# Row maxima of the scores for eight of 32 units: two key blocks as one difference, a ScalarE relu and one VectorE pass

## The chip, the cores and the metric

The kernel runs on one core of one Trainium2 chip. The engines that matter here are TensorE (PE in the profile; its weight loads are PEld), VectorE (DVE), ScalarE (ACT) and GpSimd (POOL). The metric is the device time of one execution in microseconds; lower is better. A difference is stated as a ratio of the time after to the time before.

## What is computed

The reference is a transformer block on 2048 tokens of width 512: a modulated layer norm, attention with 32 query heads of 16 columns each that share one key and one value head, an output projection with a gated residual, a second modulated layer norm, and a gated linear unit of width 1792 with a second gated residual. The part that the change touches is the softmax:

```python
q = (x @ wq).reshape(B, S, H, Dh).transpose(0, 2, 1, 3)
k = x @ wk
v = x @ wv
scores = jnp.einsum("bhqd,bkd->bhqk", q, k) * (Dh ** -0.5)
p = softmax(scores, axis=-1)
o = jnp.einsum("bhqk,bkd->bhqd", p, v)
```

The softmax needs, for every row of scores (one query of one head against all 2048 keys), the row's maximum before the exponentials are taken.

## The kernel before

**Units.** Attention is cut into 32 units (`NU`): four blocks of 512 queries, and in each block eight groups of four heads. Of the four heads two lie in partitions 0 to 63 (`a = 0`) and two in partitions 64 to 127 (`a = 1`) of the tiles that hold queries (`sst`) and keys (`kst`); the index `p` tells the two heads of one half apart. A matmul on one half uses 48 or 50 of the 64 rows there, so that a matmul of half 0 and one of half 1 can run at the same time.

**Row maxima.** They are computed a unit ahead. For each half, each head pair index `p` and each of four row groups of 128 queries (`r = 4p + t`, eight in all), the scores against a key block of 512 keys (`kc`, four of them) go into one PSUM bank (`max_mm`, tile `mx`), and VectorE takes the maximum of each row with one `tensor_reduce` (line 573) into a column of `mpart`. `max_slots(u)` lists a unit's work as slots, and each slot has one list of operations for each half. In units 1 to 31 a unit has 32 slots with one operation of kind "one" in each half. When a unit's slots are through, `max_fin` reduces `mpart` to the maxima `mm`, TensorE transposes them into `mxt` (line 597), ScalarE and VectorE split them into two fp16 rows `mt` (lines 602 and 603), and a DMA puts those under the queries in `sst`, so that the score matmul of the exponentials subtracts the maximum by itself.

Unit 0 already does it in another way. Its key blocks 2 and 3 are taken as max(s2, s3) = s2 + relu(s3 - s2). A "diff" operation puts two matmuls into one bank: the queries against `kng`, the negated keys of block 2 (a slice of the tile `kwb`), and against block 3. ScalarE writes the positive part into the tile `rel` (line 576). A "both" operation then computes s2 in another bank, and one VectorE instruction adds `rel` and reduces the sum to its maximum (line 578, a custom instruction followed by the read of its accumulator).

**Turns.** The main loop `attend` takes two turns at a time; there are 16 turns in a unit, one for each block of 128 keys. In a turn ScalarE takes four exponentials of 128x512 (`qk_exp`: a score matmul on line 620 into the tile `sc`, the exponential on line 622 into `P`), and four operations of the maxima are issued. The turn ends with `pv`, the product of the previous turn's exponentials with the values: eight matmuls on line 631 that use all 128 rows. The order inside a turn is written out by hand in strings: `NO_SIDE` when there is nothing else to compute, `FEW` when halves of a query projection (`side` on line 484 with the weights `wq`) are laid between, `MANY` for the other projections. `e0` is an exponential's matmul of half 0, `m0` a maxima slot of half 0, `x1` a side half. In `FEW` one turn takes the maxima of one half alone, four slots in a row of `r`, and the next turn those of the other; in `NO_SIDE` each turn takes two slots of both halves. The side matmuls accumulate groups of 24 halves in one bank, and after a group's end ScalarE evicts it (`qf`, line 513).

The first 30 slots of the maxima are issued before the first turn (`LEAD`), together with the loads, norms and keys. Unit 1 begins with the last six of them. The maxima of unit 8 end some 125 turns after that, so units 1 to 8 lie mostly in block 0 of the attention: first 86 turns in `FEW` order, then turns in `NO_SIDE` order.

**PSUM banks.** There are eight. `ps_mx` and `ps_sc` take the bank at the front of a queue and put it back at the end at once, so that score tiles and maxima tiles go round in a ring over all banks that nothing else holds. A matmul into a bank waits for whoever read its previous content. `pv` holds one bank for a unit, a side group one until it is evicted, and short jobs (`mxt`, sums of squares of weights on line 915) one for part of a turn.

Of the kernel before, what the change touches and what calls it, by code (L numbers as in the profile page):

```python
# [23 lines left out]
UB = H // 4  # L24
# [15 lines left out]

CHANNEL = {0: KC - 1, 3: 0, 4: 1, 6: 2}
LOW = -3.0e38
SYNC = mybir.DependencyInfo(mybir.DependencyClass.Sync, mybir.DependencyReason.DATA)


# [9 lines left out]
def adaln_mqa_glu_kernel(ctx: ExitStack, tc: tile.TileContext, x_in, wq_in, wk_in, wv_in, wo_in,  # L55
# [412 lines left out]
    class Group:  # L468
# [22 lines left out]
        def half(self, r):  # L491

            mm = self.put(r, r + 1)
            if self.rows not in (None, r):
                tc.add_manual_dep(mm.ins, sync["before"], SYNC)
            self.rows, self.turn, sync["due"] = r, now[0], True
# [30 lines left out]
    def load_q(u):  # L527
        b, g = divmod(u, UB)
        d = qd[b, g // 2].rearrange("(h e) l n -> e h l n", e=16)
        s = sst[u % 3]  # L530
        h0 = 4 * (g % 2)
        for a in range(2):
            for r, hl in ((0, 0), (1, 0), (2, 1)):
                nc.sync.dma_start(s[64 * a + 16 * r:64 * a + 16 * r + 16, :, :], d[:, h0 + a:h0 + a + 3:2, hl, :])
# [3 lines left out]
    def max_slots(u):  # L538


        if u == 0:
            slots = [[[("one", r // 4, r % 4, kc)] for _ in range(2)] for kc in range(2) for r in range(8)]
            for r in range(8):
                for a in range(2):
                    slots[-1][a].append(("diff", r // 4, r % 4, 2))
                slots.append([[("both", r // 4, r % 4, 2)] for _ in range(2)])
            return slots
        return [[[("one", r // 4, r % 4, kc)] for _ in range(2)] for kc in range(4) for r in range(8)]

    flat = [(u, i, last, step) for u in range(NU) for steps in [max_slots(u)]  # L550
            for i, step in enumerate(steps) for last in [i == len(steps) - 1]]
# [3 lines left out]
    def max_parts(u):  # L555
        if u < NU and u not in mparts:
            mparts[u] = work.tile([128, 2, 2, 4, 4], F32, name="mpart")
            if u == 0:
                nc.vector.memset(mparts[u], LOW)

    def max_mm(u, a, op):
        kind, p, t, kc = op
        s = sst[u % 3]
        m = ps_sc() if kind == "diff" else ps_mx()
        keys = [kst[:, kc * 512:(kc + 1) * 512]]
        if kind == "diff":
            keys = [kng, kst[:, (kc + 1) * 512:(kc + 2) * 512]]
        for i, w in enumerate(keys):
            nc.tensor.matmul(m, s[64 * a:64 * a + 48, p, t * 128:(t + 1) * 128], w[64 * a:64 * a + 48, :],  # L569
                             start=(i == 0), stop=(i == len(keys) - 1))  # L570
        part = mparts[u][:, a, p, t, kc:kc + 1]
        if kind == "one":
            nc.vector.tensor_reduce(part, m, axis=AX.X, op=OP.max)  # L573
        elif kind == "diff":
            r = rel[a] = work.tile([128, 512], F32, name="rel", tag="x1", bufs=6)
            relus.append(lambda: nc.scalar.activation(r, m, AF.Relu))
        else:
            nc.vector.tensor_tensor_reduce(out=rel[a], in0=m, in1=rel[a], scale=1.0, scalar=LOW, op0=OP.add,
                                           op1=OP.max, accum_out=part)

    def drain_relus():
        for f in relus:
            f()
        relus.clear()
# [3 lines left out]
    def max_fin(u):  # L588
        mms[u] = work.tile([128, 2, 8], F32, name="mm")
        nc.vector.tensor_reduce(mms[u], mparts[u].rearrange("p a q t k -> p a (q t) k"), axis=AX.X, op=OP.max)  # L590

    def max_rows(u):
        def f():
            mms[u, "b"] = ps_hold("mxt")
            p = mms[u, "b"][0:16, 0:128]
            mms[u, "p"] = p
            nc.tensor.transpose(p, mms[u].rearrange("p a c -> p (a c)"), ident)  # L597

        def g():
            p = mms[u, "p"]  # L600
            mt = [work.tile([16, 128], F16, name=f"mt{hl}") for hl in range(2)]
            nc.scalar.activation(mt[0], p, AF.Copy, scale=1.0 / 32.0)
            nc.vector.scalar_tensor_tensor(mt[1], p, 1.0 / 32.0, mt[0], op0=OP.mult, op1=OP.subtract)
            ps_give(mms[u, "b"])
            s = sst[u % 3]
            for hl in range(2):
                nc.sync.dma_start(s[48 + hl:113 + hl:64, :, :], mt[hl])
        return [(100, f, g)]
# [428 lines left out]
    def drain_posts():  # L1037
        todo = posts[:]
        posts.clear()
        if tick[0] is not None:  # L1040
            tick[0] += 1
            todo += timers.pop(tick[0], [])
        for f in todo:
            f()

    def max_half(a):
        n = mstep[a]
        mstep[a] += 1
        if n >= len(flat):
            return  # L1050
        u, i, last, ops = flat[n]
        max_parts(u)
        for op in ops[a]:
            max_mm(u, a, op)
        if a == 0:
            return
        if 0 < u < NU - 1 and i == QPRE:
            load_q(u + 1)
        if i == 12:
            max_parts(u + 1)  # L1060
        if last:
            max_fin(u)
            (_, f, g), = max_rows(u)
            later[mstep[1] + 1] = (f, g)

    def late_max():
        for at in [m for m in later if m <= mstep[1]]:
            f, g = later.pop(at)
            f()
            posts.append(g)  # L1070
            return True
        return False
# [7 lines left out]
    def open_gate(step):  # L1080
        if not fill:
            return False
        gate, group = fill[0]
        if not all(g.ended() for g in group.needs):
            return False
        if gate[0] == "h2":
            return gate[1] in h2done
        return gate[0] <= step
# [30 lines left out]
    def side_half(r, cur=cur):  # L1119
        while True:  # L1120
            if not cur:
                if cur is not second and second and second[0].turn != now[0]:
                    cur.append(second.pop())
                elif open_gate(now[0]):
                    cur.append(fill.popleft()[1])
                else:
                    return
            if not cur[0].ended():
                break
            cur.clear()  # L1130
        if cur[0].did[r] < cur[0].n:
            cur[0].half(r)

    def attend(u, kt):


        now[0] = u * NSTEP + 2 * kt
        if cur and cur[0].ended():
            cur.clear()
        side = cur[0] if cur else fill[0][1] if open_gate(now[0]) else None  # L1140
        style = NO_SIDE if side is None else FEW if side in qs else MANY
        order = [(w[0], int(w[1])) for w in style.split()]
        count = {}
        for turn in range(2):
            now[0] = u * NSTEP + 2 * (kt + turn)
            sync["before"] = sync["exp"]
            drain_posts()
            for j, (what, a) in enumerate(order):
                if j == len(order) // 2:
                    drain_posts()  # L1150
                    late_max()
                    hooks(u, 2 * (kt + turn))
                a = a if style is NO_SIDE else a ^ turn
                if what == "m" and mstep[a] >= len(flat) and style is MANY:
                    mstep[a] += 1
                    side_half(a, second)
                elif what == "m":
                    max_half(a)
                elif what == "x":
                    side_half(a)  # L1160
                else:
                    k = count[a] = count.get(a, -1) + 1
                    qk_exp(u, kt + (k // 2 if style is MANY else turn), k % 2, a)
            assert not sync["due"]
            for g in ended:
                g.finish()
            ended.clear()
            for f in ends:
                f()
            ends.clear()  # L1170
            v = u * KT + kt + turn - 1
            if v >= 0:
                pv(*divmod(v, KT))
                if v % KT == KT - 1:
                    ends.append(lambda: pv_out(u - 1))
            if not late_max() and turns:
                _, f, post = turns.popleft()
                f()
                posts.append(post)
            hooks(u, 2 * (kt + turn) + 1)  # L1180
# [22 lines left out]
    for u in range(NU):  # L1203
        if u == 1:
            side.extend(dlist)
        for kt in range(0, KT, 2):
            attend(u, kt)
# [8 lines left out]
    u = NU - 1  # L1216
# [62 lines left out]
```

## Time and profile before

| | |
|---|---|
| time, median of 3 runs (lowest to highest) | 1686.23 us (1686.07 to 1686.28) |
| time of the profiled execution | 1688.73 us |
| its span, first to last instruction | 1686.7 us |
| PE busy | 1661.1 us, 98% of the span |
| DVE busy | 1389.7 us, 82% |
| ACT busy | 1217.1 us, 72% |
| POOL busy | 517.2 us, 31% |
| chain that ended last, by engine | PE 88%, DVE 8%, ACT 2% |

The shares are means over stages with different limits. The first pass of a `pv` that lies in a turn starts at 84.45 us, the last matmul of a query projection at 302.73 us, and the maxima of unit 8 end near 403 us. Matmuls are pipelined: a matmul of 512 columns shows as 0.38 us in the profile while the next one on the same rows can start 0.22 us after it.

### The profile page before, as it was taken

To read this page: it belongs to the slowest core of one execution; us is meant where nothing else is said; L and a number is where in the kernel's file an instruction comes from. 1 tells how busy PE (TensorE), PEld (TensorE's weight loads), DVE (VectorE), ACT (ScalarE), POOL (GpSimd) and SP (SyncE) were. 2 spreads that over 40 slices of the span, in tenths; PEclk is the share of its full clock that TensorE was granted. 3 is DMA by queue.
4 is the path that set the end of the run, shared out by engine and by line. 5 is a ranking of instruction groups with operands and counts; after the bars stand their busy time and mean duration, and the time that the engine had idled before them with its cause. 6 is when DMAs were issued, how large, how long until landed. Compare 5 with 4: busy or idle time off the path is not lost.

```text
span 1686.7 us, 33353 instructions
## 1 busy us (share of the span) xinstructions
PE 1661.1 (98%) x12749; PEld 538.2 (32%) x12749; DVE 1389.7 (82%) x2364; ACT 1217.1 (72%) x2288; POOL 517.2 (31%) x691
## 2 busy tenths in 40 slices
PE   8999999999999999999999999999999999999999
PEld 3333333222223333333333333333333333334444
DVE  7899999999999999999989999999998999703110
ACT  5688888888887878777777777777777777772010
POOL 3754364626676750110040110101022111112230
PEclk9899999999999999999999999999999999999999
DMA  6112122212322210001100000000010000001000
GB/s 228 74 49 87 50 90 63 86 37 61 90 66 60 77 30 10 17 9 29 35 11 16 14 17 10 16 10 17 24 32 12 22 15 7 12 5 47 15 1 25
DMA packets 48556, 66.33 MB, mean 39 GB/s; under 512 B 14726, under 2 KB 29194, under 8 KB 48396
## 3 DMA queue, kind: packets, MB, share of 16 engines
q1 hardware_dynamic: 46812, 63.87, 12.5%
q8 instruction: 100, 1.64, 0.4%
q14 instruction: 60, 0.49, 0.1%
q10 hardware_dynamic: 1584, 0.33, 0.1%
HBM read 51.05 MB, written 8.65 MB: 35 GB/s over the span
## 4 chain that ended last, share of the span: by engine, by line
PE 88%; DVE 8%; ACT 2%; POOL 1%; issue 1%; DMA 0%; ACTq 0%; POOLq 0%
PE side L484 50%; PE pv L631 27%; DVE mpart L573 7%; PE sc L620 5%; PE mx L569 3%; ACT P L622 1%; PE misc L159 1%; PE mx L764 1%; PE part L267 0%; PE pk L274 0%; PE mxt L597 0%; POOL h L425 0%; POOL wq L425 0%; DVE bs L238 0%; ACT kwb L260 0%
## 5 line engine op out<-in xcount | busy, mean ns | idle before, releaser
L573 DVE TENSOR_REDUCE mpart<-mx 128x1 f32<-128x512 f32 x2016 | 1266.9, 684 | 95.3 <-PE mx L569 91.4
L622 ACT ACTIVATE P<-sc 128x512 f32<-128x512 f32 x2048 | 1091.6, 599 | 265.6 <-PE sc L620 221.7
L620 PE MATMUL sc<-sst,kst 50*128 50x512 f16 x2048 | 660.9, 379 | 0.8 <-DVE mpart L573 0.6
L569 PE MATMUL mx<-kst,sst 48*128 48x512 f16 x2032 | 619.7, 377 | 6.9 <-DVE mpart L573 4.2
L631 PE MATMUL pv<-P,vst 128*32 128x512 f32 x4096 | 545.3, 605 | 1.2
L484 PE MATMUL side<-h2T,wg 64*128 64x512 f16 (+1 forms) x1168 | 284.6, 378 | 0.1
L484 PE MATMUL side<-h2T,wu 64*128 64x512 f16 (+1 forms) x1166 | 282.9, 378 | 0.0
L484 PE MATMUL side<-wd,glu 64*128 64x512 f16 (+1 forms) x1008 | 234.0, 378 | 0.0
L817 POOL TENSOR_SCALAR glu<-gf 128x512 f16<-128x512 f32 x56 | 34.8, 621 | 617.7 <-DVE gf L816 539.1
L620 PEld LDWEIGHTS <-kst 50*128 50x128 f16 x2048 | 175.2, 94 | 129.5 <-issue 109.5
L569 PEld LDWEIGHTS <-sst 48*128 48x128 f16 x2064 | 185.5, 94 | 56.6 <-issue 33.5
L484 PEld LDWEIGHTS <-wg 64*128 64x128 f16 (+1 forms) x1168 | 100.7, 95 | 202.8 <-ACT P L622 94.9
L484 PEld LDWEIGHTS <-wu 64*128 64x128 f16 (+1 forms) x1166 | 100.8, 95 | 199.9 <-ACT P L622 92.2
L631 PEld LDWEIGHTS pv<-P,vst 128*32 128x32 f32 x4096 | 80.8, 108 | 218.7 <-issue 202.7
L484 PEld LDWEIGHTS <-glu 64*128 64x128 f16 (+1 forms) x1008 | 89.1, 95 | 162.9 <-ACT P L622 62.9
L816 DVE TENSOR_TENSOR gf<-side,g 128x512 f32<-128x512 f32 x56 | 38.4, 685 | 115.8 <-PE side L484 82.5
L484 PE MATMUL side<-h,wq 64*128 64x512 f16 (+1 forms) x349 | 92.8, 376 | 0.9 <-POOL wq L425 0.9
L811 ACT ACTIVATE g<-side 128x512 f32<-128x512 f32 x56 | 33.2, 593 | 81.5 <-PE side L484 81.5
L484 PE MATMUL side<-wo,och 64*128 64x512 f16 (+1 forms) x336 | 79.3, 378 | 0.0
L818 POOL TENSOR_TENSOR glu<-gf,glu 128x512 f16<-128x512 f32 x56 | 65.0, 1161 | 4.7
L200 POOL TENSOR_SCALAR rv<-st 128x1 f32<-128x1 f32 (+1 forms) x20 | 4.6, 229 | 165.0 <-DVE st L724 142.4
L665 POOL TENSOR_TENSOR oc<-oc,rr 128x512 f32<-128x512 f32 x15 | 19.1, 1273 | 109.2 <-DMA sst<-qd 94.8
(223 smaller groups left out, 815.1 us busy)
## 6 DMA issues: line engine op xcount, KB each, us to landing
wsl<-in_B_w_gate_dram SPq DMA_DIRECT2D x32, 224.0 KB
wsl<-in_B_w_up_dram SPq DMA_DIRECT2D x32, 224.0 KB
wsl<-in_B_w_down_dram SPq DMA_DIRECT2D x28, 256.0 KB
sst<-qd SPq DMA_DIRECT2D x180, 32.0 KB
oc<-ev SPq DMA_DIRECT2D x128, 32.0 KB
rr<-ri SPq DMA_DIRECT2D x16, 256.0 KB
xl<-in_A_x_dram SPq DMA_DIRECT2D x16, 256.0 KB
qd<-q SPq DMA_DIRECT2D x15, 256.0 KB
```

The costliest lines, as they stand in the source:

```text
L159: nc.tensor.matmul(pwarm, warm[:, 0:128], warm, start=True, stop=True)
L484: return nc.tensor.matmul(self.p, left[64 * r0:64 * r1], right[64 * r0:64 * r1], start=start, stop=self.ended())
L569: nc.tensor.matmul(m, s[64 * a:64 * a + 48, p, t * 128:(t + 1) * 128], w[64 * a:64 * a + 48, :], start=(i == 0), stop=(i == len(keys) - 1))
L573: nc.vector.tensor_reduce(part, m, axis=AX.X, op=OP.max)
L620: nc.tensor.matmul(t, kst[64 * a:64 * a + 50, kt * 128:(kt + 1) * 128], s[64 * a:64 * a + 50, p, :], start=True, stop=True)
L622: ex = nc.scalar.activation(ptl[u, kt, p, a], t, AF.Exp)
L631: nc.tensor.matmul(pvb[u][32 * j:32 * j + 32, :], vst[:, kt, :], ptl[u, kt, p, a], start=(kt == 0), stop=(kt == KT - 1))
L665: eng.tensor_tensor(o, o, st["r"], op=OP.mult)
L811: nc.scalar.activation(st["g", f], p, AF.Copy, scale=2.0 ** -45)
L816: nc.vector.tensor_tensor(gf, p, st["g", f], op=OP.mult)
L817: nc.gpsimd.tensor_scalar(st["glu"][:, 0, f, :], gf, 1.0, 0.0, op0=OP.mult, op1=OP.add)
L818: nc.gpsimd.tensor_tensor(st["glu"][:, 1, f, :], gf, st["glu"][:, 0, f, :], op=OP.subtract)
```

## The change

For units 1 to 8 (`DIFFS = UB`), one half of two in each row group, half `a = r % 2`, takes its key blocks 2 and 3 as unit 0 does. The four slots of a row group now come in the order 2, 0, 1, 3 of the key blocks: the diff (or, in the other half, block 2) first, then blocks 0 and 1, then the combined pass (or block 3). The tile `mpart` of these units is set to a low value first, since one of its columns is not written in such a row group, and `attend` issues the relus right behind each maxima slot.

```diff
+DIFFS = UB
...
-        return [[[("one", r // 4, r % 4, kc)] for _ in range(2)] for kc in range(4) for r in range(8)]
+        if u > DIFFS:
+            return [[[("one", r // 4, r % 4, kc)] for _ in range(2)] for kc in range(4) for r in range(8)]
+        slots = []
+        for r in range(8):
+            for kc in (2, 0, 1, 3):
+                slots.append([[("one" if a != r % 2 or kc < 2 else "diff" if kc == 2 else "both", r // 4, r % 4,
+                                min(kc, 2) if a == r % 2 else kc)] for a in range(2)])
+        return slots
...
-            if u == 0:
+            if u <= DIFFS:
                 nc.vector.memset(mparts[u], LOW)
...
                 elif what == "m":
                     max_half(a)
+                    drain_relus()
```

In the whole program PE gets 64 matmuls more (64 times a diff's two and a both's one in place of two), VectorE 64 passes fewer (64 custom instructions with their accumulator reads in place of 128 reductions) and eight memsets more, ScalarE 64 relus more.

On PE, in a turn in `FEW` order (the third `pv` to the fourth of the program), the end of the turn before the change is this; `sst_127` holds the queries whose maxima are taken, `kst` in an LDWEIGHTS row belongs to an exponential's scores and `wq` to a side half:

```order
L620 LDWEIGHTS kst
L620 MATMUL sc<-sst_126,kst 128x512
L484 LDWEIGHTS wq
L484 MATMUL side<-h_178,wq 128x512
L569 LDWEIGHTS sst_127
L569 MATMUL mx<-kst,sst_127 128x512
L484 LDWEIGHTS wq
L484 MATMUL side<-h_178,wq 128x512
L620 LDWEIGHTS kst
L620 MATMUL sc<-sst_126,kst 128x512
L569 LDWEIGHTS sst_127
L569 MATMUL mx<-kst,sst_127 128x512
```

And the same place after it:

```order
L485 MATMUL side<-h_178,wq 128x512
L577 LDWEIGHTS sst_127
L577 MATMUL sc<-kwb,sst_127 128x512
L577 LDWEIGHTS sst_127
L577 MATMUL sc<-kst,sst_127 128x512
L485 LDWEIGHTS wq
L485 MATMUL side<-h_178,wq 128x512
L628 LDWEIGHTS kst
L628 MATMUL sc<-sst_126,kst 128x512
L577 LDWEIGHTS sst_127
L577 MATMUL mx<-kst,sst_127 128x512
L639 MATMUL pv<-P,vst 32x512 x4
```

The third maxima slot of the turn, one matmul before, is two matmuls on the same rows now; nothing else in the turn has moved.

On ACT, in the first turns, the relus stand between the exponentials. Before:

```order
L622 ACTIVATE P<-sc 128x512 x24
L513 ACTIVATE qf<-side,qvs 128x512
L602 ACTIVATE mt_1555<-mxt 16x128
L622 ACTIVATE P<-sc 128x512 x16
L637 ACTIVATE ev<-pv,evs 128x512
```

After:

```order
L584 ACTIVATE rel<-sc 128x512
L630 ACTIVATE P<-sc 128x512 x5
L514 ACTIVATE qf<-side,qvs 128x512
L610 ACTIVATE mt_1575<-mxt 16x128
L630 ACTIVATE P<-sc 128x512 x7
L584 ACTIVATE rel<-sc 128x512
L630 ACTIVATE P<-sc 128x512 x4
L584 ACTIVATE rel<-sc 128x512
L630 ACTIVATE P<-sc 128x512 x5
L645 ACTIVATE ev<-pv,evs 128x512
```

Two turns of four have a relu, in the order none, none, one, one.

On PE, in a turn in `NO_SIDE` order after the change, the diff stands in the first pair of slots of every second turn:

```order
L628 LDWEIGHTS kst
L628 MATMUL sc<-sst_128,kst 128x512
L577 LDWEIGHTS sst_126
L577 MATMUL sc<-kwb,sst_126 128x512
L577 LDWEIGHTS sst_126
L577 MATMUL sc<-kst,sst_126 128x512
L577 LDWEIGHTS sst_126
L577 MATMUL mx<-kst,sst_126 128x512
L628 LDWEIGHTS kst
L628 MATMUL sc<-sst_128,kst 128x512
```

There stood two single matmuls of the two halves before; the pair of exponentials that follows comes one matmul later.

## The prediction

> **What bounds the kernel now.** I read the groups of instructions first, for durations, then busy time by window, then the timeline of single turns. The change touches only the maxima of units 1 to 8, so only the time to about 403 us can change; what follows is shifted as it stands.
>
> In the groups by line the columns are busy time, mean ns of one, idle time before.
>
> ```profile
> L573 DVE TENSOR_REDUCE mpart<-mx 128x1 f32<-128x512 f32 x2016 | 1266.9, 684 | 95.3 <-PE mx L569 91.4
> L576 ACT ACTIVATE rel<-sc 128x512 f32<-128x512 f32 x16 | 9.0, 600 | 0.9 <-PE sc L569 0.6
> L578 DVE CUSTOM_DVE_ANT_0 rel<-mx,rel 128x512 f32<-128x512 f32 x16 | 10.1, 688 | 0.7 <-ACT rel L576 0.6
> ```
>
> Unit 0 shows the new operations. The windows are the turns with side matmuls and those without (wall time, then busy PE, PEld, DVE, ACT, POOL); the third row is the `pv` matmuls of the second window.
>
> ```profile
> 84.30:304.00 219.70, 219.13 (x1779) 69.33 (x1778) 213.13 (x361) 185.08 (x360) 105.73 (x110) 1.00 0.23 69
> 304.00:401.50 97.50, 92.09 (x663) 23.25 (x661) 97.12 (x175) 82.61 (x162) 51.51 (x57) 1.00 0.20 59
> 304.00:401.50 97.50, 41.54 (x312) 6.14 (x312) 1.00 0.20 59
> ```
>
> With eight `pv` matmuls to a turn, the second window is 39 turns of 2.50 us. In the first PE is full and DVE is at 97%; in the second DVE is full. Read alone, this says that a DVE pass fewer pays in the second. The timeline says something else. First a whole turn with side matmuls, from one `pv` to the next:
>
> ```profile
> 99.83 1.07 PE L631 MATMUL pv<-P,vst 128*32 128x512 f32 x8
> 100.83 0.39 PE L620 MATMUL sc<-sst,kst 50*128 50x512 f16 x1
> 100.83 0.39 PE L569 MATMUL mx<-kst,sst 48*128 48x512 f16 x1
> 101.06 0.38 PE L484 MATMUL side<-h,wq 64*128 64x512 f16 x1
> ...
> 101.29 1.89 DVE L573 TENSOR_REDUCE mpart<-mx 128x1 f32<-128x512 f32 x3 [0.38 <-PE mx L569]
> 101.31 1.57 ACT L622 ACTIVATE P<-sc 128x512 f32<-128x512 f32 x3 [0.28 <-PE mx L569]
> ...
> 101.72 0.38 PE L569 MATMUL mx<-kst,sst 48*128 48x512 f16 x1
> 101.96 0.37 PE L620 MATMUL sc<-sst,kst 50*128 50x512 f16 x1
> 102.03 0.37 PE L569 MATMUL mx<-kst,sst 48*128 48x512 f16 x1
> ```
>
> A turn is a chain: pairs of matmuls 0.22 us apart (100.83, 101.06, ... 101.72), then 0.30 from the last maxima matmul to the `pv` (102.33), then 1.00 to the next turn. Five steps of 0.22 would put the last pair at 101.93. The exponential's matmul starts at 101.96 and the maxima matmul at 102.03: `pv` and the side group hold a bank each, six go round, and the last matmul needs the bank of the turn's first maxima, whose reduction starts at 101.29 and lasts 0.68, to 101.97. So 0.10 of each 2.50 us turn is a wait on a bank, set by the latency of one reduction and not by DVE's rate.
>
> Then a turn without side, and one some turns later:
>
> ```profile
> 336.99 0.39 PE L620 MATMUL sc<-sst,kst 50*128 50x512 f16 x2
> 337.41 2.06 ACT L622 ACTIVATE P<-sc 128x512 f32<-128x512 f32 x4 [0.31 <-PE sc L620]
> 337.43 0.38 PE L620 MATMUL sc<-sst,kst 50*128 50x512 f16 x2
> 337.73 0.70 PE L569 MATMUL mx<-kst,sst 48*128 48x512 f16 x2
> 338.36 1.06 PE L631 MATMUL pv<-P,vst 128*32 128x512 f32 x8
> 339.36 0.39 PE L620 MATMUL sc<-sst,kst 50*128 50x512 f16 x2
> ...
> 354.09 0.40 PE L620 MATMUL sc<-sst,kst 50*128 50x512 f16 x2
> 354.71 0.39 PE L569 MATMUL mx<-kst,sst 48*128 48x512 f16 x2 [0.23 <-DVE mpart L573]
> ```
>
> The last maxima matmul starts at 337.73 + 0.70 - 0.38 = 338.05. Seven banks go round, the eighth matmul needs the bank of the turn's first exponential, and that ends at 337.41 + 0.60 = 338.01. The turn is 0.42 + 0.60 + 0.04 + 0.31 + 1.00 = 2.37 us: ScalarE's latency binds it. At 354.71 DVE binds, and that turn is 2.39. The two limits are 0.02 apart, so taking DVE's away leaves the other.
>
> **The change, part by part.** There are 64 diffs. VectorE loses 64 passes: reductions of a row x4 in 2.46 to 2.48 us come every 0.60, and the custom pass is as long (688 against 684 ns). That is 38 us of DVE time, of which only what PE waited for counts.
>
> ```profile
> PEld pv L631 <- DVE mpart L573: 0.6, 1, 0.6
> ...
> PE mx L569 <- DVE mpart L573: 2.9, 13, 0.2
> PE mxt L597 <- DVE mm L590: 1.9, 3, 0.8
> L559 DVE MEMSET mpart<- x1: 112/112/112, 27.0 to 27.0; 128x64 f32 x1
> ```
>
> The first wait is from the stage with side matmuls, the next two from 304 to 412 us. The eight memsets (0.11 us each) lie in DVE's new slack and cost nothing; without that slack, 0.9 us.
>
> *Turns with side matmuls (86).* Two of four turns, 43, have a diff in their third slot. Its second matmul needs the rows of the first, so the pairs behind it come 0.22 later: the last pair at 6 x 0.22 = 1.32 after the turn's start in place of 1.20 now. The bank wait hides 0.10 of the slot, and 0.12 remains. Seven of these turns also change side groups:
>
> ```profile
> 97.97 0.39 PE L620 MATMUL sc<-sst,kst 50*128 50x512 f16 x1
> ...
> 99.04 0.37 PE L569 MATMUL mx<-kst,sst 48*128 48x512 f16 x1
> 99.05 0.39 PE L484 MATMUL side<-h,wq 64*128 64x512 f16 x1
> ...
> 99.53 0.37 PE L569 MATMUL mx<-kst,sst 48*128 48x512 f16 x1
> ```
>
> With one bank fewer the last matmul is at 1.56, 0.36 late already, and the slot is free. So 36 x 0.12 = 4.3 us; bounds 0 (all hidden) and 43 x 0.22 = 9.5. PE waits little for DVE here: I subtract the 0.6 that the row names. **+3.7.**
>
> That a matmul on the other rows doesn't overtake a blocked one shows at 99.05: the side half there, on the other rows, starts only behind the maxima matmul that waited. The Trainium skill, "TensorE: Matmul & The Clock Gate", section "Step-by-step: what each phase is for", says so too: matmuls stay in program order and only weight loads are pulled ahead. By it the sum stands; with independent row halves this term would be near 0 and the sum 4.3 lower.
>
> *Turns without side (39).* Nineteen have a diff. PE's slot is hidden: the last pair would stand at 0.88, and waits to 1.07 in any case. ScalarE has five passes there. Four in 2.06 with 0.60 for the last are 0.487 apart, so a fifth frees the engine for the next turn at 0.42 + 5 x 0.487 = 2.86, while the next turn's first score is ready at 2.37 + 0.42 = 2.79. That turn is 0.07 longer: 19 x 0.07 = 1.3. Where the eviction of `pv` also stands behind a relu, the next turn's first exponential comes some 0.4 later:
>
> ```profile
> 333.56 1.06 PE L631 MATMUL pv<-P,vst 128*32 128x512 f32 x8
> 334.34 0.71 ACT L637 ACTIVATE ev<-pv,evs 128x512 f32<-128x512 f32 x1
> ```
>
> Two such places, one of them behind other waits: 0.4; the small `mt` passes 0.2. Against it stand the waits on DVE, 2.9 + 1.9 = 4.8 us at most. Behind the first stands the 2.37 limit, 0.02 a turn away; at the unit ends `mxt` holds a bank, and a turn with one bank fewer is long in any case (1.56 + 0.30 + 1.00 = 2.86 above). I take 1.0 of the 4.8. **+0.9**, between -4.8 (all waits gone, no new one) and 19 x 0.487 = +9.3 (each relu in full).
>
> The Trainium skill, "ScalarE: Activation LUTs", section "What ACT_TABLE_LOAD costs", lets back-to-back activations overlap by about 93 ns; by that the pitch here would be 0.51 and not the 0.487 of the row. The sum by it would be 19 x 0.11 = 2.1 us more.
>
> *Before the first turn.* Two diffs of unit 1, 0 to 0.22 each: **+0.2**.
>
> Sum: 3.7 + 0.9 + 0.2 = **+4.8 us**. The span of 1686.7 becomes 1691.5, and the profiled execution (1688.73) with its 2.0 us outside the span 1693.5. It was 2.5 above the median of the runs, so the median goes from 1686.23 to 1691.0.
>
> **The rivals.**
> *DVE's rate is the limit after all* (faster). For it: DVE is busy 97.12 of 97.50 us without side. Then those turns fall from 2.50 to what ScalarE needs, 4.5 passes x 0.487 = 2.19, with 0.08 of friction 2.27: 39 x 0.23 = 9.0 less, with 3.9 more elsewhere -5.1: 1681.1. Against it: 338.05 behind 338.01. It decides if the last maxima matmul can start before the first exponential has been read. 13%.
> *Half the slots hide, and DVE's waits go* (no change). For it: 0.10 of slack per turn, and DVE's lateness may reach more turns than the rows name. 1.8 + (-1.0) + 0.2 = +1.0: 1687.2. 27%.
> *The whole slot counts* (slower). If nothing is hidden with side matmuls, 9.5 - 0.6 + 0.9 + 0.2 = +10.0: 1696.2. 8%.
> *ScalarE becomes the engine that is waited for* (slower). If each relu without side holds back the next turn by its pitch, 9.3 in place of 1.3 there: +12.8, 1699.0. Against it: ScalarE is busy 82.61 of 97.50 now, and 19 x 0.6 would make 94. The Trainium skill's rule in "ScalarE: Activation LUTs", section "Rules for kernel authors", speaks for it: relu belongs on VectorE. 10%.
> That the change moves less than it says is excluded by the order: 64 relus, 64 custom passes.
>
> **How the numbers follow.** My forecast, +4.8, has 42%; its own range is +2 to +8, 1688 to 1694. What a measurement here can tell from no change is about 0.2%, 3.4 us. Slower: forecast, whole slot and ScalarE, 60%. No change: 27%, with 1% of the DVE case, 28%. Faster: 12%. The range leaves out the far end of the DVE case and of the ScalarE case: 1682.5 to 1697.5.
>
> **What will show it.** With side matmuls, turns with two matmuls in the third slot are 2.61 to 2.62 and the others 2.50. Without side, turns stay at 2.37 with 2.44 behind each diff, the last maxima matmul still just behind the first exponential's end, and DVE idle for a tenth of the time. Turns of 2.2 to 2.3 there would make me wrong to the fast side, diff turns of 2.72 or exponentials that queue behind relus turn after turn to the slow side.

## The result, and the profile after

The changed kernel takes 1691.57 us, the median of 8 runs (1691.38 to 1696.48). The kernel before, timed beside it, takes 1686.85 us (8 runs, 1686.07 to 1690.90). The ratio is 1.003 with an interval of 1.002 to 1.004: it is slower by 4.7 us. The profiled execution after took 1691.38 us with a span of 1689.4.

The lines of the changed kernel stand eight or nine further down than before: the maxima matmul is L577 in place of L569, the reduction L581 for L573, the relu L584, the custom pass L586, a side half L485, the exponential's matmul L628 and the exponential L630, `pv` L639, the evictions `qf` L514 and `ev` L645.

The page after: busy time by engine, the chain that ended last, and three groups (busy time, mean ns of one, idle time before).

```profile
span 1689.4 us, 33645 instructions
PE 1669.6 (99%) x12813; PEld 537.2 (32%) x12813; DVE 1359.1 (80%) x2372; ACT 1245.0 (74%) x2352; POOL 517.4 (31%) x691
...
PE 90%; ACT 3%; DVE 3%; POOL 1%; issue 1%; DMA 1%; ACTq 0%; POOLq 0%; DVEq 0%
...
L581 DVE TENSOR_REDUCE mpart<-mx 128x1 f32<-128x512 f32 x1888 | 1199.8, 684 | 124.9 <-PE mx L577 120.2
L586 DVE CUSTOM_DVE_ANT_0 rel<-mx,rel 128x512 f32<-128x512 f32 x80 | 53.7, 682 | 1.6 <-ACT rel L584 0.9
```

VectorE is busy 30.6 us less than before, ScalarE 27.9 us more and TensorE 8.5 us more, and the chain has moved: VectorE's share of it went from 8% to 3%, TensorE's from 88% to 90%. The work was taken off VectorE as intended, and the program is not faster for it.

Where the 4.7 us lie is read from the turns. The length of a turn is the difference of the starts of two `pv` in the timeline, before and after, turn by turn (turn 1 is the one whose `pv` comes first). "Side" are the turns in which side halves lie; of four of them, those with a diff are the third and the fourth (T mod 4 = 3 and 0).

```
turns                                         before -> after (us each)     sum of the differences
2 to 85, side: 35 diff turns                  2.50 -> 2.62                  +4.2
               7 diff turns, group changes    2.86 -> 2.86, one 3.11          0.0
               first turn behind two diffs    2.50 -> 2.59, some 2.75       +1.7
               second turn behind them        2.50 or a little more         -0.2
86 to 125, no side: 14 turns longer           2.37 -> 2.45, one 2.43 -> 2.83  +1.3
               the others, unit ends above all  2.99 -> 2.64, 3.16 -> 2.86  -1.4
126 to 150                                    the same                       0.0
```

Together +5.6 us in the two profiled executions, and the turns with side matmuls alone are +5.75. Behind turn 150 single turns differ by up to 0.3 us either way, -0.45 in sum; the instructions are the same there. The spans of these two executions differ by 2.7 only, since the changed kernel's first `pv` came 2.5 us earlier (81.98 in place of 84.45), and that start differs from one execution to the next (last section). So the medians, 4.7 apart, and the turns can't be matched to a tenth; the lowest runs of the two kernels, 1691.38 and 1686.07, lie 5.3 apart.

First a diff turn with side matmuls, from one `pv` to the next, in the timeline of the kernel after (start, duration, engine, line, operation).

```profile
84.48 1.06 PE L639 MATMUL pv<-P,vst 128*32 128x512 f32 x8
85.48 0.39 PE L628 MATMUL sc<-sst,kst 50*128 50x512 f16 x1
...
86.36 0.38 PE L485 MATMUL side<-h,wq 64*128 64x512 f16 x1
86.37 0.38 PE L577 MATMUL sc<-kwb,sst 48*128 48x512 f16 x1
86.57 0.38 PE L628 MATMUL sc<-sst,kst 50*128 50x512 f16 x1
86.58 0.37 PE L577 MATMUL sc<-kst,sst 48*128 48x512 f16 x1
...
86.80 0.37 PE L577 MATMUL mx<-kst,sst 48*128 48x512 f16 x1
87.10 1.06 PE L639 MATMUL pv<-P,vst 128*32 128x512 f32 x8
```

The diff's two matmuls start at 86.37 and 86.58 on the same rows, and the last maxima matmul follows 0.22 later, at 86.80: 1.32 after the turn's first matmul, against 1.20 before. Then 0.30 to the `pv`, as before. The turn is 2.62 us. The other rows did not wait for the diff: the side half at 86.36 and the exponential's matmul at 86.57 stand behind both of the diff's matmuls in the program, and start 0.22 and 0.01 ahead of the second one. In this turn each half of the rows had six matmuls before; the diff's half has seven now, and the turn ends with the seventh.

Then two turns without side matmuls, the first with a diff, the second behind it.

```profile
344.59 1.07 PE L639 MATMUL pv<-P,vst 128*32 128x512 f32 x8
345.59 0.39 PE L628 MATMUL sc<-sst,kst 50*128 50x512 f16 x2
...
346.01 1.09 ACT L630 ACTIVATE P<-sc 128x512 f32<-128x512 f32 x2 [0.30 <-PE sc L628]
...
346.47 0.56 PE L577 MATMUL mx<-kst,sst 48*128 48x512 f16 x2
...
346.97 1.06 PE L639 MATMUL pv<-P,vst 128*32 128x512 f32 x8
346.99 0.60 ACT L584 ACTIVATE rel<-sc 128x512 f32<-128x512 f32 x1
...
347.46 3.07 ACT L630 ACTIVATE P<-sc 128x512 f32<-128x512 f32 x6
347.96 0.39 PE L628 MATMUL sc<-sst,kst 50*128 50x512 f16 x2
...
349.41 1.07 PE L639 MATMUL pv<-P,vst 128*32 128x512 f32 x8
```

The last maxima matmul starts at 346.47 + 0.56 - 0.38 = 346.65, and the turn's first exponential ends at 346.01 + 0.60 = 346.61: still the bank of the first exponential sets the end, and the turn is 2.38. The relu stands at 346.99, the last exponentials behind it, and the next turn is 2.44. The window from 304.9 us on (wall time, then busy PE, PEld, DVE, ACT, POOL) shows the slack that VectorE got and that nothing uses:

```profile
304.90:404.90 100.00, 98.16 (x699) 23.40 (x697) 90.81 (x181) 92.34 (x185) 52.67 (x59) 1.00 0.21 60
```

It was busy all of the time there before; now a tenth of it is idle.

### The profile page after: what moved, and what is told of

It reads as the page before. It is cut to its first block, busy times and chain, and to the rows that moved or that the text cites. A ratio compares the mean times of both kernels' runs of the same rounds, so it can differ in the third digit from the quotient of the medians.

```text
span 1689.4 us, 33645 instructions
## 1 busy us (share of the span) xinstructions
PE 1669.6 (99%) x12813; PEld 537.2 (32%) x12813; DVE 1359.1 (80%) x2372; ACT 1245.0 (74%) x2352; POOL 517.4 (31%) x691
## 4 chain that ended last, share of the span: by engine, by line
PE 90%; ACT 3%; DVE 3%; POOL 1%; issue 1%; DMA 1%; ACTq 0%; POOLq 0%; DVEq 0%
PE side L485 50%; PE pv L639 29%; PE sc L628 6%; PE mx L577 4%; ACT P L630 3%; DVE mpart L581 2%; PE sc L577 1%; PE mx L772 1%; DMA xbig<-in_A_x_dram 1%; ACT rel L584 0%; DVE bs L239 0%; PE mxt L605 0%; POOL wq L426 0%; POOL h L426 0%; PE part L268 0%
## 5 line engine op out<-in xcount | busy, mean ns | idle before, releaser
L581 DVE TENSOR_REDUCE mpart<-mx 128x1 f32<-128x512 f32 x1888 | 1199.8, 684 | 124.9 <-PE mx L577 120.2
L630 ACT ACTIVATE P<-sc 128x512 f32<-128x512 f32 x2048 | 1098.5, 602 | 243.3 <-PE sc L628 215.7
L628 PE MATMUL sc<-sst,kst 50*128 50x512 f16 x2048 | 662.4, 379 | 0.9
L577 PE MATMUL mx<-kst,sst 48*128 48x512 f16 x1968 | 608.9, 378 | 3.6 <-DVE mpart L581 1.1
L639 PE MATMUL pv<-P,vst 128*32 128x512 f32 x4096 | 545.3, 605 | 1.3
L485 PE MATMUL side<-h2T,wg 64*128 64x512 f16 (+1 forms) x1168 | 284.3, 378 | 0.0
L485 PE MATMUL side<-h2T,wu 64*128 64x512 f16 (+1 forms) x1166 | 282.9, 378 | 0.0
L485 PE MATMUL side<-wd,glu 64*128 64x512 f16 (+1 forms) x1008 | 234.2, 378 | 0.0
L628 PEld LDWEIGHTS <-kst 50*128 50x128 f16 x2048 | 177.4, 94 | 132.4 <-issue 114.0
L577 PEld LDWEIGHTS <-sst 48*128 48x128 f16 x2128 | 189.7, 94 | 46.1 <-issue 26.9
L485 PEld LDWEIGHTS <-wg 64*128 64x128 f16 (+1 forms) x1168 | 100.9, 94 | 202.6 <-ACT P L630 94.8
L485 PEld LDWEIGHTS <-wu 64*128 64x128 f16 (+1 forms) x1166 | 100.8, 95 | 200.1 <-ACT P L630 92.2
L639 PEld LDWEIGHTS pv<-P,vst 128*32 128x32 f32 x4096 | 80.8, 108 | 230.4 <-issue 214.5
L485 PEld LDWEIGHTS <-glu 64*128 64x128 f16 (+1 forms) x1008 | 89.1, 95 | 162.9 <-ACT P L630 62.9
L485 PE MATMUL side<-h,wq 64*128 64x512 f16 (+1 forms) x349 | 92.4, 377 | 0.6 <-POOL wq L426 0.4
L485 PE MATMUL side<-wo,och 64*128 64x512 f16 (+1 forms) x336 | 79.3, 378 | 0.0
L586 DVE CUSTOM_DVE_ANT_0 rel<-mx,rel 128x512 f32<-128x512 f32 x80 | 53.7, 682 | 1.6 <-ACT rel L584 0.9
```

The costliest lines, as they stand in the source:

```text
L485: return nc.tensor.matmul(self.p, left[64 * r0:64 * r1], right[64 * r0:64 * r1], start=start, stop=self.ended())
L628: nc.tensor.matmul(t, kst[64 * a:64 * a + 50, kt * 128:(kt + 1) * 128], s[64 * a:64 * a + 50, p, :], start=True, stop=True)
L630: ex = nc.scalar.activation(ptl[u, kt, p, a], t, AF.Exp)
L639: nc.tensor.matmul(pvb[u][32 * j:32 * j + 32, :], vst[:, kt, :], ptl[u, kt, p, a], start=(kt == 0), stop=(kt == KT - 1))
```

## The experiments

Each kernel computes the whole result. The first four ran on one chip beside the kernel before at 1686.49 us (29 runs), the second four on another beside 1686.67 us (13 runs).

### Which turns cost: diffs in units 1 to 5, and in units 7 and 8

The maxima of units 1 to 5 fall into the turns with side matmuls, those of units 7 and 8 into the turns without. `side_units`:

```diff
-        if u > DIFFS:
+        if u > 5:
...
-            if u <= DIFFS:
+            if u <= 5:
```

> Diffs in units 1 to 5 alone, so only in turns with side matmuls (turns 0 to 76). Bank theory (the extra matmul costs 0.12 us in each turn that has it, and side halves that wait for an exponential behind a relu cost 0.1 to 0.25 in every fourth turn): the stretch from the first pv to turn 85 is some 5 us longer than before, the turns without side are as before, in all +5 us. Rival, ScalarE's time (the loss comes where ScalarE is fullest, without side): within 1 us of before.

Measured: 1691.08 us, ratio 1.0028 (1.0018 to 1.0037). Turns 2 to 76 are 5.27 us longer than before, 77 to 150 the same within 0.01. `noside_units`:

```diff
-        if u > DIFFS:
+        if u not in (7, 8):
...
-            if u <= DIFFS:
+            if u in (0, 7, 8):
```

> Diffs in units 7 and 8 alone, so only in turns 93 to 124, without side matmuls. Bank theory: turns stay at 2.37 us, 2.45 behind a diff, and the few waits on VectorE at unit ends go: within 0.7 us of before. Rival, VectorE's rate is the limit there: turns of 2.2 to 2.3 us, 32 turns, 6 us faster than before.

Measured: 1686.70 us, ratio 0.9994 (0.9984 to 1.0004). Turns 2 to 92 are unchanged, 93 to 124 are 0.05 longer in sum (2.37 and 2.44 in turn), turn 125 is 0.30 shorter. Its window over those two units:

```profile
325.50:402.00 76.50, 74.72 (x539) 18.04 (x535) 70.01 (x143) 70.03 (x141) 35.43 (x43) 1.00 0.17 51
```

VectorE idles 6.5 of 76.5 us, TensorE 1.8. In the same window VectorE was busy 76.36 us before. So the whole cost of the change lies where side matmuls are, and where VectorE was full its relief is worth little more than the relus cost (-0.25 us over turns 93 to 125): the rate of VectorE is not what sets these turns.

### The second matmul: one_matmul

If the extra matmul is the cost, a diff of one matmul must be free. GpSimd forms the difference of the two key blocks, rounded to fp16, once, and a diff is one matmul against it (unit 0 too).

```diff
-        if b == NB - 2:
-            nc.gpsimd.tensor_scalar(kng, kst[:, cs], -1.0, 0.0, op0=OP.mult, op1=OP.add)
+        if b == NB - 1:
+            nc.gpsimd.tensor_tensor(kng, kst[:, cs], kst[:, 2 * BT:3 * BT], op=OP.subtract)
...
-            keys = [kng, kst[:, (kc + 1) * 512:(kc + 2) * 512]]
+            keys = [kng]
```

> As the change, but a diff is one matmul against the difference of the two key blocks, computed once on GpSimd; the relu and the combined pass stay. Unit 0 has it too. Bank theory: diff turns with side go from 2.62 to 2.50 us, 35 x 0.12 = 4.2 us faster than the change; what remains above before is the wait of side halves behind relus, 1.5 to 2 us. Rival, the relus and not the matmul cost: as slow as the change.

Measured: 1691.64 us, ratio 1.003 (1.002 to 1.0039), no faster than the change itself. This is a miss, and the trace gives two reasons. One lies in the turns. The first of two diff turns is back at 2.50 (0.01 us in sum over the kernel before). But the second of the two is 2.71, worse than with the extra matmul (2.41 us in sum; 2.55 and 0.31 where a side group had just changed), and the turn behind the pair is 2.82 where a group's eviction `qf` fell in (1.66 in sum). Turns 2 to 76 are 4.30 us longer than before, against 5.30 in the changed kernel. The changed kernel's turn 9 has the same wait as this last one. Its timeline, in which a bracket holds the idle time ahead of an instruction and what ended it:

```profile
98.64 0.72 ACT L514 ACTIVATE qf<-side,qvs 128x512 f32<-128x512 f32 x1
...
100.30 1.06 PE L639 MATMUL pv<-P,vst 128*32 128x512 f32 x8
...
100.65 0.68 ACT L584 ACTIVATE rel<-sc 128x512 f32<-128x512 f32 x1
101.12 2.66 ACT L630 ACTIVATE P<-sc 128x512 f32<-128x512 f32 x5
...
101.53 0.38 PE L628 MATMUL sc<-sst,kst 50*128 50x512 f16 x1
...
101.87 0.09 PEld L485 LDWEIGHTS <-wq 64*128 64x128 f16 x1 [0.46 <-ACT P L630]
...
103.05 1.07 PE L639 MATMUL pv<-P,vst 128*32 128x512 f32 x8
```

And the same turn of `one_matmul`:

```profile
102.36 0.68 ACT L584 ACTIVATE rel<-sc 128x512 f32<-128x512 f32 x1
102.84 2.65 ACT L630 ACTIVATE P<-sc 128x512 f32<-128x512 f32 x5
...
103.17 0.38 PE L628 MATMUL sc<-sst,kst 50*128 50x512 f16 x1
...
103.58 0.09 PEld L485 LDWEIGHTS <-wq 64*128 64x128 f16 x1 [0.53 <-ACT P L630]
...
104.77 1.06 PE L639 MATMUL pv<-P,vst 128*32 128x512 f32 x8
```

A turn's first side half waits for an exponential. It is a wait written into the kernel: in `half`, a side half that goes to other rows than the one before it is made to follow `sync["before"]`, the exponential issued behind the previous turn's last side half (lines 495 and 496), which is that turn's last one. In a diff turn that exponential stands behind the relu on ScalarE: the relu starts at 100.65, the exponential at 101.12 and, 0.69 us long, ends at 101.81 (five stand in that line), when the next turn is 0.51 old. The side half belongs to the second pair of matmuls, whose other one starts at 101.53; it starts at 101.87, and everything behind it on TensorE waits with it. Turn 9 is 103.05 - 100.30 = 2.75. In `one_matmul` TensorE gives ScalarE 0.12 less per diff turn, and the same wait grows: most of what was saved comes back as waiting, 2.9 of 3.9 us in turns 2 to 76. The view of waits of the changed kernel, from 84 to 307 us (total, times, longest), has the row

```profile
PEld L485 <- ACT P L630: 10.2, 32, 0.5
```

and the same view of the kernel before has one row only for the side halves, in which they wait for nothing that the profile shows:

```profile
PEld L484 <- issue: 4.1, 13, 0.4
```

The 10.2 us are idle time of the weight loader; in the turns behind two diffs 1.7 us of such waiting shows as longer turns.

The other reason lies ahead of the turns. GpSimd can form the difference only when the last key block is there, and it takes longer. The changed kernel, in which it forms the negated keys (L423 is a later pass on GpSimd):

```profile
45.89 0.62 POOL L297 TENSOR_SCALAR kwb<-kst 128x512 f16<-128x512 f16 x1 [6.85 <-DVE kst L290]
...
58.40 0.69 POOL L423 TENSOR_SCALAR kwb<-kwb,fwd 128x512 f32<-128x512 f32 x1
```

And `one_matmul`:

```profile
54.50 1.15 POOL L297 TENSOR_TENSOR kwb<-kst 128x512 f16<-128x512 f16 x1 [5.93 <-DVE kst L290]
...
60.24 0.69 POOL L423 TENSOR_SCALAR kwb<-kwb,fwd 128x512 f32<-128x512 f32 x1
```

The later pass on GpSimd is 1.84 us behind, and the first `pv` comes at 83.81 in place of 81.98, while unit 0's first relu starts at 57.2 in both. `one_matmul_late`, below, has the same 83.81. So in these profiles what the turns gave back, 1.0 us, was lost ahead of them.

### The place of the relu: late_relu

If the relu's place ahead of the turn's last exponential is the cost, it must vanish with the relu issued at the turn's end.

```diff
                 elif what == "m":
                     max_half(a)
-                    drain_relus()
...
+            drain_relus()
             assert not sync["due"]
```

> As the change, but the relu is issued at the end of its turn, behind the turn's last exponential. If side halves wait for the exponential behind the relu, the turns of 2.59 and 2.75 us that follow two diff turns go back to 2.50: 1.7 us faster than the change, diff turns stay at 2.62, and the turns without side stay at 2.37 and 2.45 (ScalarE's time is the same). Rival, the extra comes from VectorE's custom pass in those turns: as slow as the change.

Measured: 1692.61 us, ratio 1.0036 (1.0023 to 1.0048). With side matmuls it does what the theory says: the turn behind two diffs is 2.50, or 2.54 with an eviction in it (0.2 us in sum in place of 1.6), and diff turns stay at 2.62; turns 2 to 76 cost 4.05 in place of 5.30. So the rival, VectorE's custom pass, falls: it is still in those turns. The forecast for the whole kernel, 1.7 us faster than the change, was missed, since without side matmuls it loses more than that: turns 93 to 124 are 2.15 us longer, with 2.48 and 2.50 in diff pairs. There the relu now stands ahead of the next turn's first exponential, and it keeps its bank:

```profile
311.18 1.06 PE L639 MATMUL pv<-P,vst 128*32 128x512 f32 x8
312.15 0.63 ACT L584 ACTIVATE rel<-sc 128x512 f32<-128x512 f32 x1
...
312.63 2.11 ACT L630 ACTIVATE P<-sc 128x512 f32<-128x512 f32 x4
...
312.83 0.39 PE L577 MATMUL mx<-kst,sst 48*128 48x512 f16 x2 [0.27 <-ACT rel L584]
```

### Both costs away: one_matmul_late

One matmul to a diff, and the relu late in turns with side matmuls, early in those without. The edit is that of `one_matmul`, and

```diff
                     max_half(a)
-                    drain_relus()
+                    if style is NO_SIDE:
+                        drain_relus()
...
+            drain_relus()
             assert not sync["due"]
```

> The change with both of its costs with side work taken away: a diff is one matmul against the difference of the key blocks (also in unit 0), and with side work the relu is issued behind the turn's last exponential; without side work as in the change. If the cost was the extra matmul and the side halves' wait for an exponential behind a relu and nothing else, turns with side work are as before (2.50, 2.86 at group changes), and the whole is within 1 us of before. Rival, ScalarE's queue is late by the relu's time wherever it stands: diff turns or those behind them stay at 2.55 to 2.7, 2 us or more slower than before.

Measured: 1687.94 us, ratio 1.0008 (0.9999 to 1.0018). Turns 2 to 76 are 1.06 us longer than before, in place of 5.30: diff turns 2.50 (2.55 behind a group's change), the turn behind them 2.50, or 2.61 with an eviction. Turns 86 to 124 add 0.2, turn 125 takes 0.3 away. So the two costs make up 4.2 of the 5.3 us; what the other 1.1 wait for was not followed up. Taken away one at a time, the matmul gives 1.0 and the relu's place 1.3; only together they give the rest.

### Is it the bank of the first exponential: pv_early, pv_early_noside_units, both_fixed

In a turn without side matmuls the last maxima matmul waits for the bank that the turn's first exponential reads. If `pv` is issued ahead of the last two maxima slots, it doesn't stand behind that wait any more. On the kernel before:

```diff
+            v = u * KT + kt + turn - 1
             for j, (what, a) in enumerate(order):
+                if style is NO_SIDE and j == 6 and v >= 0:
+                    pv(*divmod(v, KT))
...
-            v = u * KT + kt + turn - 1
             if v >= 0:
-                pv(*divmod(v, KT))
+                if style is not NO_SIDE:
+                    pv(*divmod(v, KT))
```

> The kernel before, with pv issued ahead of the last pair of maxima slots in turns without side work, so that the last maxima matmul's wait for the first exponential's bank lies behind pv. Nothing else. The bank limit of 2.37 us is gone and VectorE's four passes at 0.597 us, 2.39, remain: turns stay at 2.38 to 2.40, the whole within 1 us of before. Rival, neither was the limit (TensorE's own order is): turns of 2.2 us, 39 to 50 of them, 7 us or more faster.

Measured: 1696.65 us, ratio 1.0056 (1.0041 to 1.0072), a miss: the turns became 2.47, not shorter; 93 to 124 are 6.8 us longer and 125 to 150 another 3.6. The same edit with the diffs of units 7 and 8:

```diff
+                if style is NO_SIDE and j == 6 and v >= 0:
+                    pv(*divmod(v, KT))
...
+        if u not in (7, 8):
```

> Both at once: pv early in turns without side work, and the change's diffs in units 7 and 8 (turns 93 to 124). If two limits stood side by side, the bank (2.37) and VectorE's rate (2.39), neither edit gains alone and both together do: turns of 2.2 to 2.3 us (ScalarE needs 4.5 x 0.487 = 2.19), 4 to 7 us faster than before. Rival, another limit at the same place (ScalarE's latency by another way, the P tiles): turns stay at 2.37 to 2.45, as before.

Measured: 1697.16 us, ratio 1.0064 (1.0045 to 1.0083), a miss as well: 2.47 with the diffs as without them. The windows of the two over those units, the first without diffs, the second with:

```profile
325.50:402.00 76.50, 71.00 (x494) 15.07 (x488) 72.70 (x130) 59.77 (x116) 29.99 (x37) 1.00 0.17 51
```

```profile
325.50:402.00 76.50, 70.22 (x492) 16.58 (x493) 64.04 (x130) 65.23 (x129) 26.40 (x34) 1.00 0.15 45
```

In the first VectorE is busy 72.70 of 76.50 us and could be the limit. In the second it is busy 64.04, ScalarE 65.23, and the turn is as long. What sets the turn is in the second one's timeline:

```profile
348.78 1.06 PE L639 MATMUL pv<-P,vst 128*32 128x512 f32 x8
...
349.78 0.39 PE L577 MATMUL mx<-kst,sst 48*128 48x512 f16 x2
...
350.21 1.89 DVE L581 TENSOR_REDUCE mpart<-mx 128x1 f32<-128x512 f32 x3 [0.31 <-PE mx L577]
...
350.56 0.76 PE L628 MATMUL sc<-sst,kst 50*128 50x512 f16 x2
351.25 1.07 PE L639 MATMUL pv<-P,vst 128*32 128x512 f32 x8
```

The first tile behind `pv` is now one of the maxima. Its reduction starts at 350.21, after 0.31 us of idle time, and ends at 350.89; the last score matmul of the turn starts at 350.56 + 0.76 - 0.38 = 350.94, and `pv` 0.31 later. The turn is 1.00 + 0.43 + 0.68 + 0.05 + 0.31 = 2.47. It was 1.00 + 0.42 + 0.60 + 0.04 + 0.31 = 2.37 with an exponential in that place. Eight tiles to a turn go through seven banks, so the eighth always waits for the reader of the first; moving `pv` only chose a slower reader. The length follows the reader's 0.60 or 0.68 us and not the load of either engine, as the bank limit says; no run changes the number of banks or of tiles, which would test it alone.

`both_fixed` puts `pv_early` on `one_matmul_late`:

```diff
+                if style is NO_SIDE and j == 6 and v >= 0:
+                    pv(*divmod(v, KT))
...
+                    if style is NO_SIDE:
+                        drain_relus()
...
+                keys = [kng]
```

> The kernel of the third run with pv early in turns without side work. Turns with side work at 2.50 as before, turns without side at 2.2 to 2.3 from turn 86 to 124: 39 x 0.2 = 6 to 8 us faster than before. If ScalarE's queue is late with side work, 2 us less of that; if the turns without side keep another limit, as before.

Measured: 1701.80 us, ratio 1.0082 (1.0063 to 1.0101). This is a miss too. Turns 2 to 76 cost 0.97, close to `one_matmul_late`, turns 93 to 124 6.9 with 2.47 in most of them as in `pv_early`. In the turns the two parts add, and neither helps the other. Turns 2 to 150 are 11.6 us longer in all; the rest of the 15 us lies ahead of them, where the profiled execution began late (first `pv` at 88.39).

No version beat the kernel before. `noside_units` and `one_matmul_late` equal it within what the measurement tells. A smaller number of tiles to a turn, or one more bank for the ring, would also show what lies beyond 2.37; neither was tried.

## Why the prediction was right, point by point

**The sign and the size.** Forecast 1691.0, measured 1691.57. In the turns the forecast was 3.7 + 0.9 = +4.6 and the traces show +5.6: one term was missing (+1.7), one too high by 1.0, and a relief of 0.6 came to 0.2. That a forecast of +4.8 stands beside medians 4.7 apart is in part luck: errors of +1.7, +0.4 and -1.0 went against each other, and the time of a single execution scatters by more than what is left.

**Turns with side matmuls, the slot.** Right, in place and size: 36 x 0.12 = 4.3 forecast, 35 turns of 0.12 and together 4.2 measured; none on the seven turns in which the groups change; the last maxima matmul at 1.32 as worked out. One step of the reasoning fails. Not all pairs behind the diff come later: on the other rows the side half and the exponential's matmul start ahead of the diff's second matmul (86.36 and 86.57 against 86.58), against the program order on which the prediction leans; the measured starts decide. What held up the side half at 99.05 was a matmul that waited for another engine to release its bank, and not one that waited for its rows. So independent row halves would not have made this term near 0: the halves do run on here, and the turn is longer all the same, since the diff's half has seven matmuls. The 0.6 us of waits for VectorE that were taken off the sum came to 0.2.

**A term that the sum lacked.** The turn behind two diffs is longer by 0.09, or by 0.25 with an eviction in it, 1.7 us in all. The prediction costed the relu only in turns without side matmuls; with side matmuls it put ScalarE at nothing and gave no reason. As far as load goes the engine has room there: busy 185.08 of 219.70 us before. What the relu moved was not the load but one exponential's end, and a side half waits for just that one. The prediction had the order of ScalarE's queue before it, but not the dependency in `half`. `late_relu` removes this term alone (0.2 in place of 1.6 in turns 2 to 76), and `one_matmul` shows that it takes up most of what TensorE saves.

**Turns without side matmuls.** The two mechanisms held: the diff's slot is hidden behind the first exponential's bank, and the turn behind a diff is 2.44 to 2.45 with 0.07 for the fifth pass of ScalarE. By the Trainium skill's overlap of about 93 ns ("ScalarE: Activation LUTs", section "What ACT_TABLE_LOAD costs") that turn would have been 0.07 + 0.11 = 0.18 longer, 2.55, by the prediction's sum, an estimate; the measured turn is nearer to the pitch of the row, and here a relu and the exponential behind it start 0.47 us apart (346.99 and 347.46). The net was mis-sized: +0.9 forecast, -0.14 measured. The costs came to 1.3 (forecast 1.9) and the relief to 1.4 (forecast 1.0). The cost was too high since only 13 turns grow by 0.05 to 0.08 and one, with an eviction, by 0.40: where a turn is long for another reason, as at a unit's end, the fifth pass adds nothing.

**Before the first turn.** +0.2 forecast; one profile of each kernel can't show it.

**The rivals.** VectorE's rate as the limit falls by `noside_units`: with an eighth of its passes gone, the turns stay 2.37. Half the slots hidden falls, since 35 of the 42 diff turns are longer by the forecast 0.12 (2.62 in most of them); the whole slot falls too, which would have made them 2.72. ScalarE as the engine that is waited for is half right: the place was wrong (with side matmuls, not without), and its price is 1.7 and not 9.3. The rule of the Trainium skill in "ScalarE: Activation LUTs", section "Rules for kernel authors", that relu belongs on VectorE, is not tested here: no run puts the relu there. What the runs show is that the pass itself is no dearer on ScalarE, 0.60 to 0.68 us against 0.68 for the pass it saves on VectorE, and that its place costs: moved behind the last exponential, with side matmuls, it costs 0.2 us in all behind the diff turns.

## What to carry to other kernels

An engine that is busy all of the time is not yet the limit: look for a second chain of nearly the same length (here 2.37 beside 2.39) before taking work from it, and lengthen or shorten the reader in that chain to see whether the turn follows. A pass that is put into another engine's queue costs what waits for the instruction behind it, so list the waits written into the kernel, not only the load. Where two costs feed the same wait, removing one shows little; remove each, and then both.

## What the runs showed of the hardware that was not expected

The extra matmul cost 3.9 us in turns 2 to 76, and taking it away gave back 1.0 of it: most of the 0.12 us by which it lengthened a turn was time that ScalarE needed for the relu.

Matmuls on the two halves of the rows do not always start in program order: one that waited for another engine held up the next one on the other rows (99.04 and 99.05 in the kernel before), one that only waited for its own rows did not (86.58, in the changed kernel, with the next one at 86.36).

Executions of one program begin unequally. The first `pv` of a turn in the profiles of `pv_early`, of the kernel before and of the changed one:

```profile
81.87 1.06 PE L631 MATMUL pv<-P,vst 128*32 128x512 f32 x8
```

```profile
84.45 1.07 PE L631 MATMUL pv<-P,vst 128*32 128x512 f32 x8
```

```profile
81.98 1.06 PE L639 MATMUL pv<-P,vst 128*32 128x512 f32 x8
```

The first two run the same instructions up to there and lie 2.6 us apart; over all profiles the start lies between 81.87 and 88.39. From there to turn 150 the turns of two kernels agree to 0.01 us wherever their instructions do (`noside_units` and the kernel before, turns 2 to 92); behind it single turns differ by up to 0.3. A difference of a few us is found turn by turn, and not in the spans.
